# The gate phase of a two-pass attention and MLP kernel: product, low part and their engines

## The chip, the cores and the metric

The kernel runs on one core of a Trainium2 chip. The core has TensorE (PE in the profile; PEld is its weight load, which runs beside the matmuls), VectorE (DVE), ScalarE (ACT), GpSimd (POOL) and SyncE (SP, which issues the DMAs). Each engine works through its own queue in order and waits at an instruction until the semaphores that it names are there. The metric is the device time of one execution in microseconds (us).

## The reference, cut to what matters

A Nystrom attention with 32 landmarks gives `x` of 4608 tokens by 512 columns; an RMS norm and a gated MLP with a hidden width of 1536 follow. The change lies in the MLP:

```python
g = xn @ w_gate
silu = g * (1.0 / (1.0 + np.exp(-g)))
val = xn @ w_val
return (silu * val @ w_out).astype(np.float32)
```

## The kernel before

**Two passes over the hidden width.** The 1536 hidden columns are cut into 12 blocks of 128. The first pass does blocks 0 to 5 for each of 8 batches of 576 tokens and stores partial outputs; the second pass does blocks 6 to 11, loads the partial outputs and adds to them. All products are made in three matmuls (high by high, high by low, low by high), so every operand exists as a high part and a low part.

**The second pass, for each batch,** is a gate phase (`seven`) and an output phase (`outs`). In the gate phase each of six blocks `f` = 0 to 5 needs gate and value for two halves of 288 tokens, a 2x2 block product, which is made from seven products instead of eight. `step(f, n)` issues product `n` (three matmuls of 288 columns into a PSUM tile p1, p2 or p7) and then the elementwise work that this product makes possible:

- n=1: ScalarE copies p1 to `u[:,0]`; n=6: ScalarE copies p1 to `u[:,1]` and takes Silu of half 0 (`s[:,0]`); n=3: ScalarE takes Silu of p1 into half 1 (`gate1`).
- n=2: VectorE forms half 0 before its Silu (`first0`). n=5: VectorE copies p1 to `u[:,2]` and adds p7 to it, which is the value of half 1 (`vv[:,1]`). n=4: VectorE adds p7 to `u[:,1]`, which is the value of half 0 (`vv[:,0]`).
- Then gate times value: `times0` (half 0, VectorE) and `times1` (half 1, GpSimd), 128x288 each.
- Then `split`: ScalarE copies the 128x576 product as the high part of `h`, and GpSimd subtracts it from the product, which leaves the low part of `h`.

The loop at the end of `seven` interleaves two blocks. Iteration `f` issues (f,1), (f-1,5), (f,2), (f,7), (f,6), (f-1,3), (f-1,4), 21 matmuls; in iteration 1, (1,2) comes before (0,5). The product of gate and value of block f-2 is issued in iteration f, and the split of block f-3 too. After iteration 5 comes (5,5); (5,3) and (5,4) are put between the first matmuls of the output phase (`ends`). Where the last block is concerned (`last`), VectorE does all of its elementwise work.

**The output phase** multiplies the six `h` tiles by `w_out` in groups of 128 tokens, 18 matmuls of 512 columns (tile `pso`) for each. The first two groups do blocks 0 to 3 each, and then blocks 4 and 5. Before the ninth block of these, the weight blocks of the next batch are mixed (`mix_blocks`, tile `pM`), except in the last batch. Sums and low parts of these weight blocks follow on VectorE, ScalarE and GpSimd.

Everything named here is kept in program order on its engine (`kept`, `mm`). Two buffers each serve `u` and `vv`, so `u` of block f is written only after the last reader of `u` of block f-2, which is (f-2,4) on VectorE.

Of the kernel before, what the change touches and what calls it, by code (L numbers as in the profile page):

```python
# [9 lines left out]
F32 = mybir.dt.float32  # L10
# [45 lines left out]
def nystrom_moe_kernel(  # L56
# [12 lines left out]
    nc = tc.nc  # L69
# [10 lines left out]
    TAIL = S % P  # L80
# [29 lines left out]
    def mm(*args, **kw):  # L110
        tc.keep_in_program_order(nc.tensor.matmul(*args, **kw))  # L111

    def kept(made):
        return tc.keep_in_program_order(made).ins
# [197 lines left out]
    def within(parts, a, z):  # L312
        for at, t in parts:
            lo, hi = max(a, at), min(z, at + t.shape[1])
            if lo < hi:
                yield lo, hi, t[:, lo - at : hi - at]
# [53 lines left out]
    hs, ends = [], []  # L370

    def new_h(f):
        if len(hs) <= f:
            hs.append(wp.tile([P, 2, TAIL + S], F32R, name=f"h{f}", tag=f"h{f}"))
        return hs[f]

    def seven(b, xb):

        banks, vv, us = {}, {}, {}
        own = {}  # L380

        def product(f, n, ps, first):
            at, of = PRODUCTS[n]
            hi, lo = (next(within(parts, at, at + 1))[2][:, 0, f % 2] for parts in own[f])
            for k, (w, x) in enumerate(((hi, xb[0]), (hi, xb[1]), (lo, xb[0]))):
                mm(
                    ps,
                    w,
                    x[:, of],
                    start=first and k == 0,  # L390
                    stop=k == 2,
                    skip_group_check=not first,
                )

        def new(f):
            pool, tag = ((pm, "pm"), (pg, "pg"))[f % 2]
            banks[f] = [pool.tile([P, 512], F32, name=f"p{n}", tag=tag)[:, :HS] for n in "127"]
            us[f] = mp.tile([P, 3, HS], F32, name="u", tag="Mhi", bufs=2)
            vv[f] = mp.tile([P, 2, HS], F32, name="vv", tag="Mlo", bufs=2)
            ss[f] = lq.tile([P, 2, HS], F32, name="s7", tag="lraw", bufs=4)  # L400
            own[f] = blocks7[b, NPAIR + f // 2]
            new_h(f)

        def gate1(f):
            silu["last"] = kept(nc.scalar.activation(ss[f][:, 1], banks[f][0], AF.Silu))  # L405

        def times1(f, eng):
            kept(eng.tensor_mul(ss[f][:, 1], ss[f][:, 1], vv[f][:, 1]))  # L408

        def first0(f):  # L410
            kept(nc.vector.tensor_add(ss[f][:, 0], us[f][:, 0], banks[f][1]))  # L411

        def times0(f):
            kept(nc.vector.tensor_mul(ss[f][:, 0], ss[f][:, 0], vv[f][:, 0]))  # L414

        def split(f, eng):
            s, h = ss[f].rearrange("p e s -> p (e s)"), hs[f]
            kept(nc.scalar.copy(h[:, 0, TAIL:], s))  # L418
            kept(eng.tensor_sub(h[:, 1, TAIL:], s, h[:, 0, TAIL:].bitcast(F32)))  # L419

        def step(f, n):
            (p1, p2, p7), u, v_, s = banks[f], us[f], vv[f], ss[f]
            last = f == NF1 - 1
            product(f, n, {1: p1, 6: p1, 5: p1, 3: p1, 2: p2, 7: p7, 4: p7}[n], n in (1, 2, 7))
            if n == 1:
                kept(nc.scalar.copy(u[:, 0], p1))  # L426
                if f > 1:
                    times1(f - 2, nc.gpsimd)
                if f > 2:
                    split(f - 3, nc.gpsimd)  # L430
            elif n == 5:
                kept(nc.vector.tensor_copy(u[:, 2], p1))  # L432
                if f == 0:
                    first0(1)
                kept(nc.vector.tensor_add(v_[:, 1], u[:, 2], p7))  # L435
                if last:
                    times0(f - 1)
                    times1(f - 1, nc.gpsimd)
                    split(f - 2, nc.gpsimd)
                    split(f - 1, nc.gpsimd)  # L440
            elif n == 2:
                if f != 1:
                    first0(f)
                if f > 1:
                    times0(f - 2)
            elif n == 6:
                kept(nc.scalar.copy(u[:, 1], p1))
                kept(nc.scalar.activation(s[:, 0], s[:, 0], AF.Silu))
            elif n == 3:
                gate1(f)  # L450
                if last:
                    times1(f, nc.vector)
            elif n == 4:
                kept(nc.vector.tensor_add(v_[:, 0], u[:, 1], p7))
                if last:
                    times0(f)
                    split(f, nc.vector)
            yield 3 * MMG

        ss = {}  # L460
        for f in range(NF1):
            new(f)
            second = ((1, 5), (0, 2)) if f > 1 else ((0, 2), (1, 5))
            for d, n in ((0, 1), *second, (0, 7), (0, 6), (1, 3), (1, 4)):
                if f >= d:
                    yield from step(f - d, n)
        yield from step(NF1 - 1, 5)
        ends.extend(step(NF1 - 1, n) for n in (3, 4))

    def mlp(wts, b, f0, an, store, part, following, after=2 * NF1):  # L470
# [742 lines left out]
    for b in range(B):  # L1213
        mix.fill(seven(b, nxt["xb"]))
        mix.fill(outs(late, b, NF1, finish, load_part, lambda b=b: next_blocks(b), NF1 - 2, 2 * NF1 - 4))
# [40 lines left out]
```

## Time and profile before

| What | Value |
|---|---|
| Median of 3 runs | 813.1 us (811.6 to 813.28) |
| The profiled execution, its own time | 811.66 us |
| Its span, first to last instruction | 809.9 us |
| TensorE busy | 777.5 us, 96% of the span |
| VectorE busy | 612.5 us, 76% |
| ScalarE busy | 418.6 us, 52% |
| GpSimd busy | 226.5 us, 28% |
| Mean granted TensorE clock | 0.992 of full speed |

The profiled execution's own time is 1.8 us more than its span. Matmuls overlap each other in the records, so a busy TensorE says little; a gap between the starts of two matmuls says more. The second pass takes the span from about 493 us to the end, with gate phases starting at about 493, 531, 572, 609, 651, 688, 730 and 767 us. All rows of one gate phase in this document are of the fifth (650 to 676 us), and those of the end are of the eighth.

### The profile page before, as it was taken

What the parts mean: (1) busy time and instruction counts of PE and PEld (TensorE: products, weight loads), DVE (VectorE), ACT (ScalarE), POOL (GpSimd) and SP (SyncE); (2) the same over time, 40 slices, a digit from 0 to 9 for tenths busy, and PEclk for the clock granted to TensorE, in tenths of its full rate; (3) what the DMA queues carried; (4) which work ended last, traced back from release to release, by engine and by line L of the source; (5) the groups of instructions that cost most, each with busy time, mean ns of one, the idle gap of its engine ahead of it and who ended that gap; (6) DMA issues with size and microseconds to landing.
All of it is one profiled execution on the core that took longest, in us unless ns stands there. A gap on an engine that the chain in (4) does not pass through costs nothing.

```text
span 809.9 us, 18024 instructions
## 1 busy us (share of the span) xinstructions
PE 777.5 (96%) x7012; PEld 618.7 (76%) x7012; DVE 612.5 (76%) x1359; ACT 418.6 (52%) x923; POOL 226.5 (28%) x235
## 2 busy tenths in 40 slices
PE   7877999999999999999999989999999999999998
PEld 5565667778778778787787959797979797979786
DVE  7999997947968678779497984867687767767682
ACT  4567565535545354545475964544455444535450
POOL 1004320110200200201110052555355435544550
PEclk9989999999999999999999999999999999999999
DMA  9956562541542523612656631424242424151412
GB/s 322 315 166 214 168 217 79 170 139 38 187 146 68 196 82 103 184 46 73 209 153 222 201 114 40 149 72 155 79 143 65 168 66 155 53 183 52 180 28 78
DMA packets 55205, 110.88 MB, mean 137 GB/s; under 512 B 5456, under 2 KB 29008, under 8 KB 55120
## 3 DMA queue, kind: packets, MB, share of 16 engines
q1 hardware_dynamic: 55120, 109.73, 40.6%
q8 instruction: 55, 0.90, 0.5%
q14 instruction: 30, 0.25, 0.1%
HBM read 73.73 MB, written 35.98 MB: 135 GB/s over the span
## 4 chain that ended last, share of the span: by engine, by line
PE 77%; DVE 13%; issue 3%; ACT 3%; DMA 2%; POOL 1%; SPq 0%; DVEq 0%; ACTq 0%; POOLq 0%
PE pso L111 35%; PE p L111 10%; PE psg L111 9%; PE psv L111 9%; PE pM L111 5%; DVE s L414 3%; PE pn L111 2%; PE sC L111 2%; PE pCV L111 1%; DVE s L411 1%; PE pO L111 1%; DVE u L432 1%; DVE lmT L572 1%; PE pss L111 1%; PE sE L117 1%
## 5 line engine op out<-in xcount | busy, mean ns | idle before, releaser
L111 PE MATMUL pso<-wo,h 128*128 128x512 f32 x648 | 160.2, 399 | 3.5 <-ACT ob L1118 3.5
L111 PEld LDWEIGHTS pso<-wo,h 128*128 128x128 f32 x648 | 119.6, 189 | 35.8 <-ACT ob L1118 4.8
L111 PE MATMUL pso<-lhio,h 128*128 128x512 f32 x432 | 139.9, 393 | 0.2
L111 PEld LDWEIGHTS pso<-lhio,h 128*128 128x128 f32 x432 | 81.0, 188 | 24.0 <-issue 5.9
L111 PE MATMUL p<-xb,Bwgv 128*128 128x288 f32 x560 | 92.1, 297 | 0.5
L111 PE MATMUL psg<-an,Mhi 128*128 128x288 f32 x384 | 85.1, 305 | 1.9 <-ACT an L986 1.2
L111 PE MATMUL psv<-an,Mhi 128*128 128x288 f32 x384 | 83.4, 301 | 1.2 <-DVE s L504 1.2
L111 PE MATMUL pso<-lloo,h 128*128 128x512 f32 x216 | 84.2, 390 | 0.0
L111 PEld LDWEIGHTS p<-xb,Bwgv 128*128 128x128 f32 x560 | 81.3, 188 | 3.0 <-DVE vv L435 2.4
L111 PE MATMUL p<-xb,Bwo 128*128 128x288 f32 x392 | 74.2, 300 | 1.6 <-ACT u L426 1.6
L111 PEld LDWEIGHTS psg<-an,Mhi 128*128 128x128 f32 x384 | 62.0, 189 | 13.7 <-DVE WT L893 5.0
L649 POOL TENSOR_TENSOR tA<-tA,mA 128x576 f32<-128x576 f32 x16 | 18.8, 1196 | 169.0 <-DVE mA L648 169.0
L419 POOL TENSOR_TENSOR h<-s,h 128x576 fp32r<-128x576 f32 x40 | 57.4, 1436 | 27.7 <-ACT h L418 27.7
L111 PEld LDWEIGHTS psv<-an,Mhi 128*128 128x128 f32 x384 | 62.2, 189 | 3.5 <-DVE s L504 1.4
L111 PEld LDWEIGHTS p<-xb,Bwo 128*128 128x128 f32 x392 | 58.8, 188 | 7.6 <-ACT u L426 4.6
L503 ACT ACTIVATE s<-psg 128x288 f32<-128x288 f32 x96 | 39.5, 411 | 41.7 <-PE psg L111 41.1
L111 PE MATMUL psv<-an,Mlo 128*128 128x288 f32 x192 | 58.7, 306 | 0.0
L1118 ACT COPY ob<-pso 128x512 f32<-128x512 f32 x36 | 21.1, 589 | 72.6 <-PE pso L111 59.7
L111 PE MATMUL psg<-an,Mlo 128*128 128x288 f32 x192 | 58.4, 304 | 0.1
L408 POOL TENSOR_TENSOR s<-s,vv 128x288 f32<-128x288 f32 x40 | 36.8, 919 | 75.0 <-ACT s L405 55.5
L1179 DVE TENSOR_TENSOR obl<-obl,pso 128x512 f32<-128x512 f32 x36 | 24.7, 686 | 41.8 <-PE pso L111 41.8
L414 DVE TENSOR_TENSOR s<-s,vv 128x288 f32<-128x288 f32 x48 | 55.6, 1159 | 0.3
(192 smaller groups left out, 1558.0 us busy)
## 6 DMA issues: line engine op xcount, KB each, us to landing
xb<-ad SPq DMA_DIRECT2D x16, 1008.0 KB, 6.0
qk<-in_q_dram SPq DMA_DIRECT2D x16, 576.0 KB, 4.8
qk<-in_k_dram SPq DMA_DIRECT2D x16, 576.0 KB, 6.1
pd<-ob SPq DMA_DIRECT2D x36, 256.0 KB, 3.6
ad<-t SPq DMA_DIRECT2D x64, 144.0 KB, 1.8
obl<-pd SPq DMA_DIRECT2D x36, 256.0 KB, 2.8
out_dram<-obl SPq DMA_DIRECT2D x36, 256.0 KB, 2.2
vt<-in_v_dram SPq DMA_DIRECT2D x16, 512.0 KB, 5.7
```

Of the source, the lines that this page charges most:

```text
L111: tc.keep_in_program_order(nc.tensor.matmul(*args, **kw))
L117: tc.keep_in_program_order(nc.tensor.transpose(*args))
L408: kept(eng.tensor_mul(ss[f][:, 1], ss[f][:, 1], vv[f][:, 1]))
L411: kept(nc.vector.tensor_add(ss[f][:, 0], us[f][:, 0], banks[f][1]))
L414: kept(nc.vector.tensor_mul(ss[f][:, 0], ss[f][:, 0], vv[f][:, 0]))
L419: kept(eng.tensor_sub(h[:, 1, TAIL:], s, h[:, 0, TAIL:].bitcast(F32)))
L432: kept(nc.vector.tensor_copy(u[:, 2], p1))
L503: silu["last"] = nc.scalar.activation(s[:, cols], banks[0], AF.Silu).ins
L572: fixed["sums", b] = nc.vector.tensor_reduce(lmT[:, z], loaded[b, g][z].rearrange("p h (m c) -> p h m c", c=LM), axis=AX.X, op=ALU.add,)
L649: nc.gpsimd.tensor_sub(tA, tA, mA.unsqueeze(2).broadcast_to([P, NB, M]))
L1118: nc.scalar.copy(ob, ps)
L1179: kept(nc.vector.tensor_add(ob, ob, ps))
```

## The change

The halves' two products become one operation of 128x576 on GpSimd (`times`), in iteration f as before. `split` becomes two functions: `high` (ScalarE's copy, where it was) and `low` (the subtraction, now always on VectorE, behind `first0` of step n=2). `first0(1)` is moved behind the value add of (0,5). For the last blocks, GpSimd makes the product of block 4, VectorE makes both low parts of blocks 3 and 4, and the two halves of block 5 stay two operations on VectorE. Line numbers move: `times` has line 411 after the change, `first0` 408, `high` 414, `low` 418, the copy and the adds of VectorE 431, 432 and 453.

```diff
-        def times1(f, eng):
-            kept(eng.tensor_mul(ss[f][:, 1], ss[f][:, 1], vv[f][:, 1]))
-
         def first0(f):
             kept(nc.vector.tensor_add(ss[f][:, 0], us[f][:, 0], banks[f][1]))
 
-        def times0(f):
-            kept(nc.vector.tensor_mul(ss[f][:, 0], ss[f][:, 0], vv[f][:, 0]))
-
-        def split(f, eng):
+        def times(f, eng, e=slice(0, 2)):
+            kept(eng.tensor_mul(ss[f][:, e], ss[f][:, e], vv[f][:, e]))
+
+        def high(f):
+            kept(nc.scalar.copy(hs[f][:, 0, TAIL:], ss[f].rearrange("p e s -> p (e s)")))
+
+        def low(f):
             s, h = ss[f].rearrange("p e s -> p (e s)"), hs[f]
-            kept(nc.scalar.copy(h[:, 0, TAIL:], s))
-            kept(eng.tensor_sub(h[:, 1, TAIL:], s, h[:, 0, TAIL:].bitcast(F32)))
+            kept(nc.vector.tensor_sub(h[:, 1, TAIL:], s, h[:, 0, TAIL:].bitcast(F32)))
...
             if n == 1:
                 kept(nc.scalar.copy(u[:, 0], p1))
                 if f > 1:
-                    times1(f - 2, nc.gpsimd)
+                    times(f - 2, nc.gpsimd)
                 if f > 2:
-                    split(f - 3, nc.gpsimd)
+                    high(f - 3)
             elif n == 5:
                 kept(nc.vector.tensor_copy(u[:, 2], p1))
+                kept(nc.vector.tensor_add(v_[:, 1], u[:, 2], p7))
                 if f == 0:
                     first0(1)
-                kept(nc.vector.tensor_add(v_[:, 1], u[:, 2], p7))
                 if last:
-                    times0(f - 1)
-                    times1(f - 1, nc.gpsimd)
-                    split(f - 2, nc.gpsimd)
-                    split(f - 1, nc.gpsimd)
+                    times(f - 1, nc.gpsimd)
+                    for i in (f - 2, f - 1):
+                        high(i)
+                        low(i)
             elif n == 2:
                 if f != 1:
                     first0(f)
-                if f > 1:
-                    times0(f - 2)
+                if f > 2:
+                    low(f - 3)
...
             elif n == 3:
                 gate1(f)
                 if last:
-                    times1(f, nc.vector)
+                    times(f, nc.vector, slice(1, 2))
             elif n == 4:
                 kept(nc.vector.tensor_add(v_[:, 0], u[:, 1], p7))
                 if last:
-                    times0(f)
-                    split(f, nc.vector)
+                    times(f, nc.vector, slice(0, 1))
+                    high(f)
+                    low(f)
```

On VectorE, at the start of the fifth gate phase, the rows of before are these; the first three hold `first0(0)`, the copy of (0,5) and `first0(1)`, and the names s_8340 and s_8362 are the gate tiles of blocks 0 and 1.

```order
L411 TENSOR_TENSOR s_8340<-u,p_8336 128x288
L432 COPY u<-p_8335 128x288
L411 TENSOR_TENSOR s_8362<-u,p_8358 128x288
L435 TENSOR_TENSOR vv<-u,p_8337 128x288
L454 TENSOR_TENSOR vv<-u,p_8337 128x288
```

In the change the same place reads as follows (tile numbers differ; s_8320 and s_8342 are blocks 0 and 1).

```order
L408 TENSOR_TENSOR s_8320<-u,p_8316 128x288
L431 COPY u<-p_8315 128x288
L432 TENSOR_TENSOR vv<-u,p_8317 128x288
L408 TENSOR_TENSOR s_8342<-u,p_8338 128x288
L453 TENSOR_TENSOR vv<-u,p_8317 128x288
```

The value add of (0,5) has moved ahead of `first0(1)`.

On VectorE, iteration 5 of the same gate phase and what follows it, before; L411 is `first0(5)`, L414 `times0`, L408 `times1` of the last block, L419 the low part of block 5, and s_8434, s_8473 and s_8512 are blocks 3, 4 and 5.

```order
L432 COPY u<-p_8468 128x288
L435 TENSOR_TENSOR vv<-u,p_8470 128x288
L411 TENSOR_TENSOR s_8512<-u,p_8508 128x288
L414 TENSOR_TENSOR s_8434<-s_8434,vv 128x288
L454 TENSOR_TENSOR vv<-u,p_8470 128x288
L432 COPY u<-p_8507 128x288
L435 TENSOR_TENSOR vv<-u,p_8509 128x288
L414 TENSOR_TENSOR s_8473<-s_8473,vv 128x288
L408 TENSOR_TENSOR s_8512<-s_8512,vv 128x288
L454 TENSOR_TENSOR vv<-u,p_8509 128x288
L414 TENSOR_TENSOR s_8512<-s_8512,vv 128x288
L419 TENSOR_TENSOR h_1303<-s_8512,h_1303 128x576
```

In the change the same place reads as follows; L418 is `low`, and s_8377, s_8413, s_8451 and s_8489 are blocks 2 to 5.

```order
L432 TENSOR_TENSOR vv<-u,p_8448 128x288
L408 TENSOR_TENSOR s_8489<-u,p_8485 128x288
L418 TENSOR_TENSOR h_978<-s_8377,h_978 128x576
L453 TENSOR_TENSOR vv<-u,p_8448 128x288
L431 COPY u<-p_8484 128x288
L432 TENSOR_TENSOR vv<-u,p_8486 128x288
L418 TENSOR_TENSOR h_1137<-s_8413,h_1137 128x576
L418 TENSOR_TENSOR h_1235<-s_8451,h_1235 128x576
L411 TENSOR_TENSOR s_8489<-s_8489,vv 128x288
L453 TENSOR_TENSOR vv<-u,p_8486 128x288
L411 TENSOR_TENSOR s_8489<-s_8489,vv 128x288
L418 TENSOR_TENSOR h_1303<-s_8489,h_1303 128x576
```

In the iteration, the product of half 0 has given way to a low part of twice the size, of the block before it; behind the iteration, two low parts stand ahead of the last block's products where one product stood.

On GpSimd, the end of the same gate phase before, blocks 2 to 4:

```order
L408 TENSOR_TENSOR s_8397<-s_8397,vv 128x288
L419 TENSOR_TENSOR h_889<-s_8362,h_889 128x576
L408 TENSOR_TENSOR s_8434<-s_8434,vv 128x288
L419 TENSOR_TENSOR h_978<-s_8397,h_978 128x576
L408 TENSOR_TENSOR s_8473<-s_8473,vv 128x288
L419 TENSOR_TENSOR h_1137<-s_8434,h_1137 128x576
L419 TENSOR_TENSOR h_1235<-s_8473,h_1235 128x576
```

And in the change the whole gate phase, blocks 0 to 4:

```order
L411 TENSOR_TENSOR s_8320<-s_8320,vv 128x576
L411 TENSOR_TENSOR s_8342<-s_8342,vv 128x576
L411 TENSOR_TENSOR s_8377<-s_8377,vv 128x576
L411 TENSOR_TENSOR s_8413<-s_8413,vv 128x576
L411 TENSOR_TENSOR s_8451<-s_8451,vv 128x576
```

GpSimd has five operations in a gate phase where it had ten, and none of them reads `h`. The queues of TensorE, ScalarE and SyncE hold the same operations in the same order as before.

## Rows read from the trace of the kernel before

**Rows 1.** Page: busy time by engine, then shares of the chain that ended last.

```profile
PE 777.5 (96%) x7012; PEld 618.7 (76%) x7012; DVE 612.5 (76%) x1359; ACT 418.6 (52%) x923; POOL 226.5 (28%) x235
...
PE 77%; DVE 13%; issue 3%; ACT 3%; DMA 2%; POOL 1%; SPq 0%; DVEq 0%; ACTq 0%; POOLq 0%
```

**Rows 2.** Groups by form, weight loads of the gate products: last fields idle time before, releasers.

```profile
L111 PEld LDWEIGHTS p<-xb,Bwgv 128*128 128x128 f32 x560 | 81.3, 188 | 3.0 <-DVE vv L435 2.4
L111 PEld LDWEIGHTS p<-xb,Bwo 128*128 128x128 f32 x392 | 58.8, 188 | 7.6 <-ACT u L426 4.6 <-DVE u L432 2.4
```

**Rows 3.** Timeline of TensorE, fifth gate phase: start, length, operation, count, idle before.

```profile
650.72 5.16 PE L111 MATMUL p<-xb,Bwgv 128*128 128x288 f32 x35
...
655.84 0.83 PE L111 MATMUL p<-xb,Bwgv 128*128 128x288 f32 x5
...
661.67 1.72 PE L111 MATMUL p<-xb,Bwo 128*128 128x288 f32 x10
...
663.89 1.89 PE L111 MATMUL p<-xb,Bwo 128*128 128x288 f32 x13
666.00 1.85 PE L111 MATMUL p<-xb,Bwo 128*128 128x288 f32 x12 [0.23 <-ACT u L426]
667.69 0.40 PE L111 MATMUL pso<-lhio,h 128*128 128x512 f32 x1
...
668.83 0.39 PE L111 MATMUL pso<-lhio,h 128*128 128x512 f32 x1
669.13 0.66 PE L111 MATMUL p<-xb,Bwo 128*128 128x288 f32 x3
669.63 0.39 PE L111 MATMUL pso<-lhio,h 128*128 128x512 f32 x1
```

**Rows 4.** Chain in order of time, fifth gate phase: start, length (us), what.

```profile
665.55 0.41 ACT u L426
```

**Rows 5.** Timeline of VectorE, same stretch.

```profile
657.67 0.45 DVE L414 TENSOR_TENSOR s<-s,vv 128x288 f32<-128x288 f32 x1
...
661.72 0.44 DVE L454 TENSOR_TENSOR vv<-u,p 128x288 f32<-128x288 f32 x1
662.09 0.45 DVE L432 COPY u<-p 128x288 f32<-128x288 f32 x1
662.64 0.45 DVE L435 TENSOR_TENSOR vv<-u,p 128x288 f32<-128x288 f32 x1
...
663.50 1.58 DVE L414 TENSOR_TENSOR s<-s,vv 128x288 f32<-128x288 f32 x1
665.00 0.44 DVE L454 TENSOR_TENSOR vv<-u,p 128x288 f32<-128x288 f32 x1
```

**Rows 6.** Timeline of GpSimd, same stretch.

```profile
663.33 1.43 POOL L419 TENSOR_TENSOR h<-s,h 128x576 fp32r<-128x576 f32 x1 [0.86 <-ACT h L418]
664.72 1.02 POOL L408 TENSOR_TENSOR s<-s,vv 128x288 f32<-128x288 f32 x1
```

**Rows 7.** Timeline of TensorE where the last batch's gate work ends.

```profile
790.64 1.03 PE L111 MATMUL pso<-lhio,h 128*128 128x512 f32 x2
...
792.53 0.39 PE L111 MATMUL pso<-lloo,h 128*128 128x512 f32 x1
```

**Rows 8.** Timeline of the weight loads at the same place.

```profile
791.18 0.19 PEld L111 LDWEIGHTS pso<-lhio,h 128*128 128x128 f32 x1 [0.57 <-ACT h L418]
...
791.97 0.30 PEld L111 LDWEIGHTS pso<-lhio,h 128*128 128x128 f32 x2 [0.49 <-DVE h L419]
```

**Rows 9.** Groups by line: count | busy us, mean ns of one.

```profile
L419 POOL TENSOR_TENSOR h<-s,h 128x576 fp32r<-128x576 f32 x40 | 57.4, 1436 | 27.7 <-ACT h L418 27.7
L408 POOL TENSOR_TENSOR s<-s,vv 128x288 f32<-128x288 f32 x40 | 36.8, 919 | 75.0 <-ACT s L405 55.5 <-PE p L111 19.0
L419 DVE TENSOR_TENSOR h<-s,h 128x576 fp32r<-128x576 f32 x8 | 6.1, 759 | 5.9 <-ACT h L418 5.9
L418 ACT CAST h<-s 128x576 fp32r<-128x576 f32 x48 | 32.4, 675 | 40.0 <-DVE s L414 40.0
```

## Prediction

> **What bounds the kernel now.** I read the page first. TensorE is 96% busy and holds 77% of the chain that ended last, but VectorE holds 13% of it [rows 1]. So somewhere TensorE waits for VectorE, and only that can be won. The groups of the weight loads say where: in the second pass the loads of the gate products stood idle behind VectorE's value add L435 and copy L432, 2.4 us each, and behind ScalarE's copy L426, 4.6 us [rows 2]. That is 0.3, 0.3 and 0.6 us in each of eight gate phases, so one phase can stand for all.
>
> TensorE's timeline of the fifth phase gives the loss in issue time. Undisturbed, 44 matmuls go from 655.84 to 661.67, 0.1325 us each, so the 21 of an iteration need 2.78 us. From 650.72 to 667.69 lie 120 matmuls: 15.90 us of work in 16.97, so 1.07 us are lost. Of these, 0.23 fall between 661.67 and 663.89 (15 matmuls, 1.99 of 2.22 us), 0.39 between 663.89 and 666.00 (13 matmuls, 1.72 of 2.11), 0.10 in the slow restart to 667.69 (12 matmuls, 1.59 of 1.69), and what is left, 0.35, lies before 655.84, at the wait for L435. Behind the phase, (5,3) starts late: 668.83 to 669.13 is 0.30 where five matmuls from 667.69 took 0.228 each, and its three matmuls take 0.50 instead of 0.40, together 0.17 [rows 3]. Sum: 1.24 us a phase.
>
> ScalarE's copy, which is named for the two middle losses, is only the messenger. It needs the `u` buffer that L454 reads last; L454 ended at 665.44, the copy starts at 665.55 and ends at 665.96, and TensorE goes on at 666.00 [rows 3 to 5]. VectorE is the late one: from L454 to L454 it takes 665.00 - 661.72 = 3.28 us [rows 5], 0.5 more than TensorE needs for an iteration.
>
> Why 3.28? `times0` (L414) takes 0.45 us alone, at 657.67, but 1.58 at 663.50 [rows 5]. GpSimd's low part L419 had begun at 663.33 and ends at 664.76, and L414 ends 0.32 us later, at 665.08 [rows 5, 6]. The reverse shows too: GpSimd's product at 664.72 takes 1.02 us and so ends 0.66 us after L414. Operations of VectorE that read PSUM, L454 at 665.00 among them, keep their 0.44 us beside it [rows 5]. So an operation of VectorE with both inputs in SBUF stands still until GpSimd's ends. The SBUF — State Buffer page of the Trainium skill, section "Who interferes with whom", states this as an exclusive lock for the whole instruction, in which the loser fully blocks; the trace agrees, with 1.58 us against 0.45.
>
> In the last batch there is no mixing of weights to cover the end of the gate work: from 790.64 to 792.53 five matmuls of 0.228 take 1.89 us, 0.75 too long [rows 3, 7], behind the high and the low part of block 5 [rows 8].
>
> **The change, step by step.** *GpSimd:* each block gets one product of 128x576 in place of a product of 0.92 us and a low part of 1.44 us [rows 9]. No row shows this product. If the second half were free it would take 0.92, as two halves 1.84; I take 1.44, that of the subtraction of the same size with two inputs on the same engine.
>
> *VectorE:* `times0` goes, `low` (128x576) comes. Alone it takes 0.76 us [rows 9]. Blocked, L414 ended 0.32 behind GpSimd where alone it takes 0.45, so 0.13 of it had passed; `low` would end 0.76 - 0.13 = 0.63 behind GpSimd.
>
> Now one iteration, with TensorE unhindered and (f,1) starting at 0. Three matmuls need 0.40 to issue, the last lasts 0.29, and a handover takes 0.05 to 0.1 (665.96 to 666.00, 665.44 to 665.55), so a product can be read 0.6 us after its start. (f-2,4) began at -0.40: the value add of half 0 runs 0.20 to 0.65. GpSimd's product can then run 0.75 to 2.19. (f-1,5) starts at 0.40: VectorE's copy 1.00 to 1.45, the value add 0.55 behind the copy's start (662.09 to 662.64, it waits for the copy), 1.55 to 2.00, `first0` 0.37 behind it (661.72 to 662.09, the distance of neighbours), 1.92 to 2.37, and `low` from 2.29 to 3.05. At 2.29 GpSimd has ended (2.19), and `high`, which needs only the product of the iteration before, ran on ScalarE for 0.68 us behind the copy of p1, at about 1.1 to 1.8. The next value add can begin at 0.20 + 2.78 = 2.98, and VectorE is ready at 2.97. If `low` does meet the product, it ends 0.63 behind it.
>
> The worst round of VectorE, with `low` always blocked and nothing else waited for: GpSimd starts 0.55 after the value add starts and ends at 1.99; `low` ends at 2.62, and the next add starts 0.08 before that, so a round is 2.54. Unblocked it is 0.37 + 0.55 + 0.37 + 0.37 + 0.68 = 2.34. Both are under TensorE's 2.78, where 3.28 was above. TensorE's least margin is that of (f-1,4), which starts at 2.39 and needs the second value add, done at 2.00: 0.39 us, 0.3 after the handover. ScalarE's copies, Silus and `high` keep their places, and the copy is no longer held. So the middle losses, 0.23 + 0.39 + 0.10, go, and the 0.17 of (5,3) too, which waited for the same late VectorE: 0.89 us a phase.
>
> *`first0(1)` behind the value add:* copy, `first0`, value add took two distances of 0.37, 0.74; copy and value add together take 0.55. The loss of 0.35 shrinks by 0.19.
>
> *The end of a phase.* In the frame of iteration 5, (5,5) starts at 2.78. GpSimd's product of block 4 runs about 3.5 to 5.0; VectorE's `low(3)` follows the copy and value add at 4.3, is blocked, and ends at 5.6. TensorE needs it at 3.18 + three blocks of 0.686 + two products of 0.80 + 0.46 = 6.5: 0.9 us of cover. `high(4)` to 5.7, `low(4)` to 6.5 (needed at 9.9), the product of half 1 to 6.9, the value add to 7.2, the product of half 0 to 7.8, `high(5)` to 8.5, `low(5)` to 9.3. TensorE wants `low(5)` at 3.18 + 9 x 0.686 + 0.80 + 0.46 = 10.6 without the weight mixing. So in the last batch the 0.75 us go as well; if that cover of 1.3 us were gone, this one batch would pay for what is missing.
>
> *Sum:* 8 x (0.89 + 0.19) + 0.75 = 9.4 us; at most, with the whole loss of the value add, 8 x 1.24 + 0.75 = 10.7. The profiled execution took 811.66 us, so it would take 802.3, and at least 801.0. The median of the runs is 1.4 us above it and would come to 803.7; I forecast 803.0, between the two.
>
> The GPSIMD Engine Reference of the Trainium skill, section "Engine selection", speaks against giving the product to GpSimd: it counts it about half as fast as VectorE for two inputs. The rows say the same of the subtraction, 1.44 us against 0.76 [rows 9]. It would decide if GpSimd's time lay on the path; by the schedule it doesn't, and the sum stays.
>
> **The rivals.** (1) The lock moves with the new operation. `low` is the longer one, and if GpSimd's product starts late, because a Silu on ScalarE is late, it meets `low` in each iteration and the margin of 0.3 us is used up. The near meeting of 2.19 and 2.29 speaks for it, the round of 2.54 against it. With half of the gain left: 813.1 - 4.7 = 808.4 in the median.
>
> (2) ScalarE's copy is late by itself, not by VectorE. Then 0.72 us a phase stay, and the gain is 8 x (0.19 + 0.17) + 0.75 = 3.6: 809.5. That 4.6 us of idle time carry ScalarE's name speaks for it [rows 2], the 0.11 us between L454's end and the copy's start against it.
>
> (3) The change doesn't do what it says: TensorE gains in the gate phase, and waits as much longer at the next one for weight blocks from VectorE, ScalarE and GpSimd. Then it stays at 813. Against it: these blocks are released by TensorE's own matmuls, and they move with them.
>
> (4) Slower: GpSimd's product costs much more than the subtraction. A round is 0.55 + D + 0.63 - 0.08 = D + 1.10, so from D = 2.18 us it is as long as the 3.28 of before. At D = 2.9, twice the subtraction, a round is 4.0, 0.72 worse in three iterations of eight phases: 17 us, 830. Only the price bars it: two halves together cost 1.84 at most [rows 9].
>
> **How the numbers follow.** My forecast 0.78, rival 1 0.09, rival 2 0.05, rival 3 0.04, rival 4 0.04. A change under 0.2% (1.6 us) can't be told from none here. So faster 0.92 (forecast, 1 and 2), same 0.04 (3), slower 0.04 (4). The range goes from 800.8, the largest sum with 0.2 us of spread, to 807.5, which takes in the smaller share of rival 1.
>
> **What would show it.** Right: VectorE's round from value add to value add at 2.78 in iterations 3 to 5; `low` at 0.76 to 0.9; GpSimd's product at about 1.44; no idle time of the gate weight loads behind ScalarE's copy, about 0.1 us a phase behind the value add; in the last batch no wait for block 5. Wrong: `low` at 1.5 us or more, GpSimd's product above 2 us, or new waits at `pso` for `h`.

## The result, and the profile after

The median after the change is 802.6 us (4 runs, 802.3 to 802.9); before it is 813.0 us (4 runs, 811.6 to 813.28). The ratio is 0.9875, with a 95% interval of 0.9858 to 0.9892: faster by 1.25%. The forecast was 803.0 us. The profiled execution took 802.3 us, which is what the sum had given for it, and its span is 800.5 us. The single executions lie 0.6 us apart here and 1.7 us before.

The weight loads of the gate products, grouped as in [rows 2] (the last field is idle time before them):

```profile
L111 PEld LDWEIGHTS p<-xb,Bwgv 128*128 128x128 f32 x560 | 81.3, 188 | 1.2
L111 PEld LDWEIGHTS p<-xb,Bwo 128*128 128x128 f32 x392 | 58.9, 188 | 1.2
```

The 3.0 and 7.6 us of before are down to 1.2 each, and no releaser is named any more. TensorE's timeline in the fifth gate phase answers to [rows 3]:

```profile
646.61 4.92 PE L111 MATMUL p<-xb,Bwgv 128*128 128x288 f32 x35
...
657.32 1.49 PE L111 MATMUL p<-xb,Bwo 128*128 128x288 f32 x10
658.65 0.42 PE L111 MATMUL p<-xb,Bwgv 128*128 128x288 f32 x2
...
659.31 3.48 PE L111 MATMUL p<-xb,Bwo 128*128 128x288 f32 x25
662.63 0.40 PE L111 MATMUL pso<-lhio,h 128*128 128x512 f32 x1
...
663.79 0.39 PE L111 MATMUL pso<-lhio,h 128*128 128x512 f32 x1
664.02 0.56 PE L111 MATMUL p<-xb,Bwo 128*128 128x288 f32 x3
664.41 0.39 PE L111 MATMUL pso<-lhio,h 128*128 128x512 f32 x1
```

From 646.61 to 662.63 the 120 matmuls take 16.02 us, where 16.97 stood before and 15.90 is the undisturbed rate. The other phases agree: each of the eight takes 16.02 to 16.11 us, and took 16.96 to 17.06 before. The 25 matmuls from 659.31 run through at 0.133 us each, where 0.49 us was lost before (0.39 in the wait and 0.10 in the slow restart). (5,3) starts 0.23 us after the matmul in front of it and takes 0.39: no loss. VectorE and GpSimd in the same stretch, answering to [rows 5, 6], first VectorE:

```profile
656.86 0.46 DVE L453 TENSOR_TENSOR vv<-u,p 128x288 f32<-128x288 f32 x1
...
658.95 0.75 DVE L418 TENSOR_TENSOR h<-s,h 128x576 fp32r<-128x576 f32 x1
659.64 0.46 DVE L453 TENSOR_TENSOR vv<-u,p 128x288 f32<-128x288 f32 x1
...
663.76 2.21 DVE L418 TENSOR_TENSOR h<-s,h 128x576 fp32r<-128x576 f32 x2
```

and GpSimd:

```profile
657.49 1.44 POOL L411 TENSOR_TENSOR s<-s,vv 128x576 f32<-128x576 f32 x1 [1.35 <-DVE vv L453]
```

The same two operations as groups of the whole second pass (count, busy us, mean ns of one):

```profile
L411 POOL TENSOR_TENSOR s<-s,vv 128x576 f32<-128x576 f32 x40 | 57.3, 1433 | 102.0 <-DVE vv L453 100.7 <-ACT s L405 1.3
L418 DVE TENSOR_TENSOR h<-s,h 128x576 fp32r<-128x576 f32 x48 | 40.8, 850 | 7.4 <-ACT h L414 6.4
```

From value add to value add VectorE takes 2.78 us, TensorE's own pace, where it took 3.28. GpSimd's product ends at 658.93 and `low` begins at 658.95, unblocked, in 0.75 us. Only `low(3)` behind the phase is blocked, as worked out: the two at 663.76 take 2.21 us together. In all eight phases `low(3)` takes 1.33 or 1.34 us and ends 0.61 or 0.62 behind GpSimd's product, and the other 40 take 0.75 or 0.76; so the mean is 0.85. The chain of waits shows the last batch (start, length, what). Before, 61 matmuls behind the wait for block 5 ended it:

```profile
791.16 0.77 DVE h L419
791.97 14.11 PE pso L111 x61
```

After:

```profile
759.43 16.02 PE p L111 x120
...
778.32 18.40 PE pso L111 x81
```

The last 81 output matmuls run in one piece, 0.227 us each. The wait of 0.75 us [rows 7, 8] is gone.

Of the 10.4 us between the medians, the second pass gives 9.7. From the first gate matmul of the first phase to the end of the span it took 316.7 us before and 307.0 after. The other 0.7 us are spread between executions and not the change: the two profiled ones differ by 9.4 us (811.66 and 802.3), and their first pass, which is the same code, ended at 493.2 us before and 493.5 after. In all profiled executions of this study it ended between 492.3 and 495.5 us. So I compare second passes below, beside the times; each comes from one execution.

### The profile page after: what moved, and what is told of

It is laid out like the page before. It is cut to its first block, busy times and chain, and to the rows that moved or that the text cites. A ratio compares the mean times of both kernels' runs of the same rounds, so it can differ in the third digit from the quotient of the medians.

```text
span 800.5 us, 17919 instructions
## 1 busy us (share of the span) xinstructions
PE 773.2 (97%) x7012; PEld 622.0 (78%) x7012; DVE 589.9 (74%) x1359; ACT 418.3 (52%) x923; POOL 190.3 (24%) x195
## 4 chain that ended last, share of the span: by engine, by line
PE 87%; DVE 5%; DMA 4%; ACT 2%; issue 1%; POOL 1%; SPq 0%; DVEq 0%; ACTq 0%; POOLq 0%
PE pso L111 36%; PE p L111 17%; PE psg L111 10%; PE psv L111 9%; PE pM L111 5%; PE pn L111 2%; DMA wrawv<-in_moe_w_val_dram 2%; PE sC L111 2%; PE pCV L111 1%; PE pO L111 1%; PE pss L111 1%; DVE lmT L572 1%; PE pW L111 1%; DMA wrawg<-in_moe_w_gate_dram 1%; PE sE L117 1%
## 5 line engine op out<-in xcount | busy, mean ns | idle before, releaser
L411 POOL TENSOR_TENSOR s<-s,vv 128x576 f32<-128x576 f32 x40 | 57.3, 1433 | 102.0 <-DVE vv L453 100.7
L111 PE MATMUL p<-xb,Bwo 128*128 128x288 f32 x392 | 70.1, 295 | 0.0
L504 DVE TENSOR_TENSOR s<-s,psv 128x288 f32<-128x288 f32 x96 | 42.2, 446 | 13.6 <-PE psv L111 9.2
L418 DVE TENSOR_TENSOR h<-s,h 128x576 fp32r<-128x576 f32 x48 | 40.8, 850 | 7.4 <-ACT h L414 6.4
```

The costliest lines, as they stand in the source:

```text
L411: kept(eng.tensor_mul(ss[f][:, e], ss[f][:, e], vv[f][:, e]))
L418: kept(nc.vector.tensor_sub(h[:, 1, TAIL:], s, h[:, 0, TAIL:].bitcast(F32)))
L504: nc.vector.tensor_mul(s[:, cols], s[:, cols], banks[1])
```

## The experiments

All ratios are to the kernel before. "Second pass" is measured as above.

**The changed kernel again (e1_after_again).**

> The changed kernel once more, as the base for the other runs of this chip. Expected: 802.6 us where before takes 813.0, a ratio of 0.987.

Measured: 803.3 us, ratio 0.9877 (0.986 to 0.9894), second pass 307.1 us.

**The order alone (e2_order_only),** on the kernel before:

```diff
                 kept(nc.vector.tensor_copy(u[:, 2], p1))
+                kept(nc.vector.tensor_add(v_[:, 1], u[:, 2], p7))
                 if f == 0:
                     first0(1)
-                kept(nc.vector.tensor_add(v_[:, 1], u[:, 2], p7))
```

> The kernel before with one line moved: first0(1) behind the value add of (0,5), nothing else. My theory (the lock gives most of the gain, the order a small part): TensorE's wait for that add shrinks from 0.33 to 0.12 us in each of eight phases, so about 1.8 us less than before, 811.2. Rival (the order gives most of it): near 803.

Measured: 810.75 us, ratio 0.9975 (0.9966 to 0.9984), second pass 314.8 us, 1.9 less than before. The idle time behind VectorE's value add is gone from the weight loads, that behind ScalarE's copy and VectorE's copy stays (4.5 and 2.3 us). So the order gives 0.25% and what is left, about 1%, comes from the rest of the change.

**Halves again (e3_halves),** on the changed kernel:

```diff
-                    times(f - 2, nc.gpsimd)
+                    times(f - 2, nc.gpsimd, slice(1, 2))
...
+                if f > 1:
+                    times(f - 2, nc.vector, slice(0, 1))
                 if f > 2:
                     low(f - 3)
...
-                    times(f - 1, nc.gpsimd)
+                    times(f - 1, nc.vector, slice(0, 1))
+                    times(f - 1, nc.gpsimd, slice(1, 2))
```

> The changed kernel, but with the product of gate and value split again as before: half 0 on VectorE behind first0, half 1 on GpSimd; low stays on VectorE. VectorE now does more per block than in either kernel (0.45 us more than after the change). My theory: GpSimd's half product of 0.81 us has ended before VectorE's two operations with both inputs in SBUF come up, so none is blocked; VectorE's round is 0.37 + 0.55 + 0.37 + 0.37 + 0.37 + 0.68 = 2.71 us, just under TensorE's 2.78: 802.6 to 803.6. Rival (VectorE's load decides): more load than before, so no better than 811.

Measured: 804.1 us, ratio 0.9895 (0.988 to 0.9909), second pass 307.3 us. The time is half a microsecond above what I had expected, the second pass 0.2 above the changed kernel's. VectorE's groups of the second pass:

```profile
L418 DVE TENSOR_TENSOR h<-s,h 128x576 fp32r<-128x576 f32 x48 | 36.2, 754 | 7.4 <-ACT h L414 6.4
L411 DVE TENSOR_TENSOR s<-s,vv 128x288 f32<-128x288 f32 x56 | 25.4, 454 | 0.3
```

All 48 low parts take 0.754 us and all 56 half products 0.454. VectorE has 40 operations more than in either kernel, and the gain stays. What cost the time before was not VectorE's load. The busy time of the page does not show this, since an operation that stands still counts as busy: VectorE is busy for 612.5 us before, 599.4 here and 589.9 in the changed kernel, and of the 612.5 about 42 are the 56 half products beyond 0.454 us each.

**The engines exchanged (e5_swap),** on the changed kernel; in the end of the phase too, except for block 5:

```diff
-        def low(f):
+        def low(f, eng=nc.gpsimd):
...
-                if f > 1:
-                    times(f - 2, nc.gpsimd)
                 if f > 2:
                     high(f - 3)
+                    low(f - 3)
...
-                if f > 2:
-                    low(f - 3)
+                if f > 1:
+                    times(f - 2, nc.vector)
```

> The changed kernel with the two engines exchanged: VectorE makes the whole product of 128x576, GpSimd the whole low part of 128x576; each engine has as many operations of the same size as after the change. My theory (the lock, so it matters when they meet): GpSimd's low part starts 1.6 us after VectorE's value add, just before VectorE's product is up, and blocks it until 0.63 us after its own end; VectorE's round is 1.61 + 1.43 + 0.63 - 0.08 = 3.6 us, longer than the 3.28 of before: 815 to 822 us. Rival (GpSimd's load was the cause, which fell from 2.36 to 1.44 us a block): the same load as after the change, so 802.6.

Measured: 811.0 us, ratio 0.998 (0.9971 to 0.999), second pass 315.1 us. With the same operations on each engine as the changed kernel has, or nearly, the whole gain but for the order's part is gone. GpSimd's load as the cause falls with this. But the size was not what I expected, and the timeline says why, first VectorE's, then GpSimd's:

```profile
658.27 0.46 DVE L452 TENSOR_TENSOR vv<-u,p 128x288 f32<-128x288 f32 x1
...
660.30 1.69 DVE L411 TENSOR_TENSOR s<-s,vv 128x576 f32<-128x576 f32 x1
661.91 0.44 DVE L452 TENSOR_TENSOR vv<-u,p 128x288 f32<-128x288 f32 x1
...
663.49 0.75 DVE L411 TENSOR_TENSOR s<-s,vv 128x576 f32<-128x576 f32 x1
664.41 0.45 DVE L452 TENSOR_TENSOR vv<-u,p 128x288 f32<-128x288 f32 x1 [0.16 <-PE p L111]
```

```profile
659.94 1.43 POOL L418 TENSOR_TENSOR h<-s,h 128x576 fp32r<-128x576 f32 x1 [13.77 <-ACT h L414]
663.57 1.97 POOL L418 TENSOR_TENSOR h<-s,h 128x576 fp32r<-128x576 f32 x1 [2.20 <-DVE s L408]
```

In the first round GpSimd is there 0.36 us earlier, VectorE's product ends 0.62 behind it, and the round, from 658.27 to 661.91, is 3.6 us, as expected. In the next, VectorE is late, so its product comes 0.08 us before GpSimd's low part, and now GpSimd waits (1.97 us) and VectorE's round is 2.5. The lock goes to whoever comes first, and a late VectorE comes first. My estimate had every round blocked.

**An idle operation on GpSimd (e6_dummy_half, e8_dummy_full, e7_dummy_memset),** on the changed kernel, behind each `times(..., nc.gpsimd)`:

```diff
+        def idle_op(f):
+            junk = lp.tile([P, HS], F32, name="junk", tag="junk", bufs=1)
+            kept(nc.gpsimd.tensor_mul(junk, vv[f][:, 1], vv[f][:, 1]))
```

The full one multiplies both halves into a tile of `[P, 2, HS]`; the memset writes a tile of `[P, 864]` instead. No later work reads these tiles, but the two products read `vv`, whose buffer can be written again only behind them; the memset doesn't.

> The changed kernel with one more operation on GpSimd behind each product: a product of 128x288 with two inputs in SBUF into a tile that nobody reads (0.81 us). Nothing waits for its data. My theory: GpSimd holds the lock for 1.44 + 0.81 = 2.25 us, low is blocked to 0.63 us behind it, VectorE's round is 3.35 us as before the change: 809.5 to 813.5, low at 1.3 us or more. Rival (only data matter): 802.6.

> As the run with the extra half product, but the extra operation of GpSimd is a memset of 128x864, which reads nothing and lasts about as long (0.8 us). My theory, with the lock only between operations that read two inputs on VectorE and operations that read on GpSimd: nothing is blocked, 802.2 to 803.4, low at 0.75 us. Rival (any work of GpSimd stops VectorE's two-input operations, or GpSimd's load decides): as with the extra half product, 809.5 to 813.5.

> The changed kernel with an extra product of 128x576 on GpSimd behind each product, into a tile that nobody reads, so that GpSimd holds 2.88 us on end: the rival of the prediction in which GpSimd's product costs twice the subtraction. My theory: VectorE's round is 4.0 us, low about 2 us, and the time 823 to 831, where the prediction had named 830 for it. Rival (only data matter): 802.6.

Measured: half product 807.4 us, ratio 0.9932 (0.9917 to 0.9947); memset 805.4, 0.9906 (0.9889 to 0.9922); full product 810.35, 0.9971 (0.9959 to 0.9983). None lies where it was expected. In the kernel with the full product, VectorE:

```profile
658.41 0.45 DVE L459 TENSOR_TENSOR vv<-u,p 128x288 f32<-128x288 f32 x1 [0.68 <-PE p L111]
...
660.50 1.68 DVE L422 TENSOR_TENSOR h<-s,h 128x576 fp32r<-128x576 f32 x1
662.11 0.44 DVE L459 TENSOR_TENSOR vv<-u,p 128x288 f32<-128x288 f32 x1
...
665.76 0.44 DVE L459 TENSOR_TENSOR vv<-u,p 128x288 f32<-128x288 f32 x1
...
667.41 0.98 DVE L422 TENSOR_TENSOR h<-s,h 128x576 fp32r<-128x576 f32 x1
668.31 0.44 DVE L459 TENSOR_TENSOR vv<-u,p 128x288 f32<-128x288 f32 x1
```

and GpSimd:

```profile
660.43 1.14 POOL L415 TENSOR_TENSOR junk<-vv 128x576 f32<-128x576 f32 x1
...
666.35 1.42 POOL L411 TENSOR_TENSOR s<-s,vv 128x576 f32<-128x576 f32 x1 [1.13 <-DVE vv L459]
667.73 1.66 POOL L415 TENSOR_TENSOR junk<-vv 128x576 f32<-128x576 f32 x1
```

The idle operation does block `low`, although nobody waits for its data: it ends at 661.57, `low` at 662.18, 0.61 behind it, as the working had it (0.63). But two operations of GpSimd are not one hold of the lock. At 667.41 `low` is waiting already when the product ends at 667.77; it goes in between, ends at 668.39, and the idle operation waits for it (1.66 us instead of 1.14). My rounds of 3.35 and 4.0 us had counted both operations as one hold in every round. They had also taken the idle operations too long: unblocked these take 0.66 us (half) and 1.14 (full), not 0.81 and 1.44, so GpSimd had 1.43 + 1.14 = 2.57 us of work on end and not 2.88. Where `low` is blocked through, the round is what the prediction's D + 1.10 gives for D = 2.57, 3.67: the rounds here are 3.70 and 3.65 us. The third is 2.55. This phase is the worst of the eight; in the other seven only the first of these three rounds is blocked through, and the others take about 2.55 and 3.0 us. The full product's second pass is 313.9 us, 6.8 more than the changed kernel's, where I had expected 20 to 28.

The memset, VectorE first, then GpSimd:

```profile
658.48 0.75 DVE L422 TENSOR_TENSOR h<-s,h 128x576 fp32r<-128x576 f32 x1
```

```profile
658.39 0.82 POOL L415 MEMSET junk<- 128x864 f32 x1
```

The two lie on top of each other, and `low` takes 0.75 us: an operation of GpSimd that only writes does not block it. The loads of the gate weights waited no longer than in the changed kernel (1.3 and 1.2 us), and yet the second pass took 309.4 us, 2.3 more. The chain of waits of this kernel has its last 81 output matmuls at

```profile
781.48 18.84 PE pso L111 x81
```

that is 0.2326 us each instead of 0.2272. Neither theory had that. The tile itself was the suspect, since it moves what lies behind it in memory.

**The place in memory (e9_pad_only, e10_memset_aligned, e11_half_aligned),** on the runs with the memset, the memset and the half product:

```diff
-            junk = lp.tile([P, 864], F32, name="junk", tag="junk", bufs=1)
-            kept(nc.gpsimd.memset(junk, 0.0))
+            lp.tile([P, 864], F32, name="junk", tag="junk", bufs=1)
...
-            junk = lp.tile([P, 864], F32, name="junk", tag="junk", bufs=1)
+            junk = lp.tile([P, 832], F32, name="junk", tag="junk", bufs=1)
...
-            junk = lp.tile([P, HS], F32, name="junk", tag="junk", bufs=1)
-            kept(nc.gpsimd.tensor_mul(junk, vv[f][:, 1], vv[f][:, 1]))
+            junk = lp.tile([P, 320], F32, name="junk", tag="junk", bufs=1)
+            kept(nc.gpsimd.tensor_mul(junk[:, :HS], vv[f][:, 1], vv[f][:, 1]))
```

> The changed kernel with a tile of 3456 bytes a partition (864 f32) reserved in the pool of the second pass's weights, and nothing that writes or reads it. In the run with the memset no wait was added, but TensorE's matmuls of 512 columns followed each other at 0.232 us instead of 0.227. Theory (place in memory): the reserved tile moves the tiles behind it by a size that is no multiple of 256 bytes, and the matmuls that stream these are slower: 0.232 again, about 2.2 us more than the changed kernel, 805. Rival (the memset's own writes slow the matmuls): 803, 0.227.

> As the run with the memset, but of 832 f32 instead of 864, 3328 bytes, which is 13 times 256. Theory (place in memory): matmuls of 512 columns at 0.227 us again, and since GpSimd's memset blocks nothing, the time of the changed kernel, 802.6 to 803.4. Rival (the memset's writes): 0.232, 805.

> As the run with the extra half product, but its tile is reserved with 1280 bytes, five times 256, instead of 1152. What is left against the changed kernel is then the lock alone. From the earlier run with the place in memory taken out: gate phases about 1.9 us longer in sum, 804.6 to 805.4, matmuls of 512 columns at 0.227 us. Rival (there was no lock in that run, only the place in memory): 802.6 to 803.4.

Measured: the reserved tile alone 805.3 us, ratio 0.9907 (0.9892 to 0.9922), second pass 309.4; the memset of 832 elements 803.5, 0.9881 (0.9866 to 0.9895), 306.9; the half product with 1280 bytes 804.5, 0.9897 (0.988 to 0.9913), 308.5. The last two lie 0.1 us outside what was expected, one above and one below. The last output matmuls of the first, and then of the second:

```profile
782.34 18.84 PE pso L111 x81
```

```profile
779.34 18.39 PE pso L111 x81
```

So the place in memory alone cost 2.3 us of the second pass (309.4 against 307.1). Without it the run with the memset is 2.5 us shorter and the one with the half product 2.7 (311.2 with 1152 bytes), and the memset itself costs nothing. VectorE's low parts in the memset's and the half product's run, as groups:

```profile
L422 DVE TENSOR_TENSOR h<-s,h 128x576 fp32r<-128x576 f32 x48 | 40.7, 848 | 7.3 <-ACT h L418 6.4
L422 DVE TENSOR_TENSOR h<-s,h 128x576 fp32r<-128x576 f32 x48 | 52.0, 1084 | 7.4 <-ACT h L418 6.4
```

Against the changed kernel's 307.1 the lock itself costs 1.4 us for the half product; the ratios of the two (0.9897 and 0.9877) can't be told apart, and it is the traces that show it. The 120 gate matmuls of a phase, added up over the eight phases, take 128.3 us in the changed kernel, 128.2 and 128.3 with the memset in either place, and 130.0 with the half product in either place. With the full product they take 134.7. Its tile has 2304 bytes, nine times 256, and its output matmuls kept 0.227 us. TensorE waits there behind ScalarE's copy as it did before the change, and the value add L437 of each phase's last block waits 0.3 us for the idle product to have read `vv`:

```profile
L111 PEld LDWEIGHTS p<-xb,Bwo 128*128 128x128 f32 x392 | 59.2, 188 | 6.3 <-ACT u L429 5.1
L437 DVE TENSOR_TENSOR vv<-u,p 128x288 f32<-128x288 f32 x48 | 21.8, 455 | 6.3 <-POOL junk L415 2.5 <-DVE u L436 0.5
```

So of its 6.8 us the 6.4 in the gate phases go with the blocked `low`; how much of the rest is the lock's and how much the buffer's was not separated.

**One copy on ScalarE (e4_act_copy),** on the changed kernel:

```diff
-                kept(nc.vector.tensor_copy(u[:, 2], p1))
+                if f == 0:
+                    kept(nc.scalar.copy(u[:, 2], p1))
+                else:
+                    kept(nc.vector.tensor_copy(u[:, 2], p1))
```

> The changed kernel with the copy of p1 after (0,5) on ScalarE instead of VectorE, in block 0 alone. What is left of TensorE's waits in the gate phase is 0.12 us for the value add of block 0, which stands 0.49 us behind VectorE's copy. ScalarE copies in 0.40 us and is free there. Theory: the wait goes, 8 x 0.12 = 0.9 us less than the changed kernel. Rival: the handover between the engines costs what the copy saves, no change.

Measured: 802.9 us, ratio 0.9873 (0.9858 to 0.9889), second pass 306.4 us. The idle time of the weight loads on `Bwgv` falls from 1.2 to 0.9 us and the second pass by 0.7. The times of this kernel and of the changed one (0.9877) can't be told apart, so it is not shown that it beats the change.

## Why the prediction was right

**VectorE's round.** The main step held: `low` follows the end of GpSimd's product instead of running into it, and VectorE's round no longer exceeds TensorE's 2.78 us. Blocked behind the phase, it ends 0.61 us behind GpSimd's product, where 0.63 had been worked out. The near meeting was nearer than worked out, 0.02 us instead of 0.10, because GpSimd started 0.63 us behind the value add's start and not 0.55. Had it been blocked, a round would by the working have been 2.54 us, or 2.62 with the measured start, and cost nothing. One round of another run bears this out as far as it goes: in the last phase of e9 GpSimd started 0.28 us later, `low` was blocked and took 0.87 us, and the phase's 120 matmuls took 16.01 us as elsewhere.

**The terms.** The middle losses and that of (5,3), 0.89 us a phase, went in full. The value add was to give 0.19 and gave 0.23: 0.12 us of the 0.35 are left (16.02 against 15.90). VectorE's add follows the copy by 0.49 us there, not by 0.55. The last batch gave its 0.75. Sum 8 x (0.89 + 0.23) + 0.75 = 9.7, which is what the second pass lost; the prediction had 9.4. The order alone measured 1.9 (8 x 0.23 = 1.8). That the forecast of 803.0 us lies so near the median of 802.6 is partly luck: by its own sum the median would have come to 803.7, and the forecast was put between that and the profiled execution's 802.3.

**The costs that no row had shown.** GpSimd's product of 128x576 takes 1.433 us on average; taken was 1.44, the subtraction's, which stood in for a product that no row showed. `low` takes 0.75 unblocked; 0.76 was taken.

**What the trace of before had made of the cause.** That the lock, and not load, decides, is shown by four runs together: more load on VectorE costs nothing (e3), the same load at other times costs the gain (e5), an operation without a reader costs time if it reads (e8, clear of the noise, and e11 by its trace), and none if it only writes (e10). The trace of before agrees: of the 48 `times0` of the second pass, 32 end 0.31 or 0.32 us behind a GpSimd operation, and the other 16 take 0.45 or 0.46 us. The SBUF — State Buffer page of the Trainium skill, section "Who interferes with whom", draws this line between GpSimd operations that read SBUF and those that only write it; the memset agrees, with `low` at 0.75 us under it.

**What was wrong, off the path.** The price of rival 4, 830 us for twice the time on GpSimd, was not tested as one operation of 2.9 us. As two operations of 2.57 us together it is 810: D + 1.10 holds for a round that is blocked through, but the step "in three iterations of eight phases" fails, since VectorE comes between the two and a late VectorE comes first. For a single long operation it stays open. The same error made e5, e6 and e8 come out lower than expected, e6 and e8 also because the idle operations were shorter than taken.

## What to carry to other kernels

When VectorE works on two SBUF inputs, look at what GpSimd runs at that moment: a duration that jumps from 0.45 to 1.6 us and ends a fixed time behind a GpSimd operation (0.31 us here) points to a lock, and the remedy here was to place the two one behind the other, not to take load off. Work out the schedule of one round, and ask whether the worst round, with every meeting blocked, is still shorter than the bounding engine's; if it is, the order need not be exact. When a dummy or a buffer is added for an experiment, reserve it alone as a control; in this kernel a size that is a multiple of 256 bytes a partition cost nothing. And ask what the dummy reads: a buffer that it reads comes free only behind it.

## What the runs showed that I had not expected

A reserved tile of 3456 bytes a partition that nothing touches (and likewise one of 1152) slowed the matmuls of 512 columns behind it from 0.2272 to 0.2326 us, 2.3 us over the second pass; tiles of 3328, 1280 and 2304 bytes, which are multiples of 256, did not. Both slow sizes leave 128 bytes over a multiple of 256; other remainders were not tried. Which of the moved tiles matters was not separated. And two GpSimd operations back to back are not one hold: a waiting VectorE operation goes in between (`low` at 667.41, 0.98 us).
